# Attention's loads in another order: v one group of heads later, q and k one group sooner

## The chip, the cores and the metric

One core of a Trainium2 chip runs the whole program. The metric is the device time of one execution in microseconds; three runs of the kernel before are given below, and one more was taken by the hardware profiler.

## What is computed

The reference is an attention with sigmoid in place of softmax, followed by a maximum over three products and an output product:

```python
def _attn_ref(q, k, v):                      # 8 batches, 12 heads, 448 positions, 64 wide
    S = q.shape[2]
    scores = np.matmul(q, k.transpose(0, 1, 3, 2)) / np.sqrt(q.shape[-1]) - np.log(S)
    attn = 1.0 / (1.0 + np.exp(-scores))
    return np.matmul(attn, v)

def _moe_ref(x, w1, w2, w3, w_out):          # x: 3584 tokens of 768; weights 768 x 768
    h = np.maximum(np.maximum(x @ w1, x @ w2), x @ w3)
    return h @ w_out
```

## The kernel before, in words

The program has two stretches. The first, `attention` (lines 238 to 410), works through 24 groups of four heads: `fours` (line 335) lists 8 batches by 3 groups. A group has two pairs of heads; each pair has one tile qk of 128 partitions by 896 (two heads of 64 rows, q and k side by side), 448 KB. All four heads share one tile v of 448 KB. The second stretch (lines 416 to 555) does the four products in a Strassen-like scheme of seven block products, operands split in two float32r parts (`PRODUCTS`, `product`); its weights are decoded from 64-bit words, a part of them during attention.

Most instructions are pinned to program order (`pin`), so each engine's row is the order in which the code is written. One turn n of attention's loop (lines 365 to 408) puts these in the rows:

- SP (the load and store queue): `load(n + 1)`, that is the two qk tiles (line 270) and then v (line 275) of the next group; the raw weight words of a later decode, wraw (line 134); in half of the decodes a store of the decoded words, w_dram (line 173); from turn 9 on, for twelve turns, a block of attention's own output, xs (line 190); at the end the two stores of the finished group, x_dram (line 350).
- TensorE: `last_scores` of group n (line 313; positions 384 to 447 of all four heads, read from the unsplit qk tiles), the three score chunks of the first pair (line 301; two go to ps_s, the third to ps_av through `accumulator`), the three chunks of the second pair (all to ps_s), and then the weighing of group n - 1 with v: 24 matmuls of `weigh` (line 321) and 8 of `last_weigh` (line 330), all into ps_av.
- ScalarE: a sigmoid of each score chunk (line 280; the tile is named last for `last_scores`, else a), with the two steps of one weight decode (lines 144 and 145) between the first and the second pair.
- VectorE: up to two weight splits (lines 122 and 123), `qk_split` of the next group's first pair (hi, line 289, and lo, line 290), the decode's four steps (lines 146 to 155), `qk_split` of the next group's second pair, and the copies m of group n - 1 out of ps_av (line 349), which the stores of line 350 wait for.
- GpSimd: sums of weight blocks (line 110) and of x blocks (line 199).

Group 0 is different: its first pair isn't split, and its turn has two calls of `decode`, of which the first only issues the first two wraw loads.

Buffers decide when a load can go. There are four qk tiles (line 242), that is two groups, and two v tiles (line 244). There is one ps_av, so the third chunk of a group can't be written until the copies m of the group weighed before have read it, and the weighing can't begin until the third chunk's sigmoid has. There are three ps_s tiles, and two each of hi and lo, which the scores of a pair hold to their end. A load that has to wait for its buffer stands in SP's row, and what is behind it stands too. In `load(n + 1)` the qk tiles are those of group n - 1, which was last read at the beginning of turn n - 1; the v tile is that of group n - 1, which is weighed at the end of turn n.

Of the kernel before, what the change touches and what calls it, by code (L numbers as in the profile page):

```python
# [34 lines left out]
def attention_then_maxout(  # L35
# [84 lines left out]
    def w_split(q, name, r, copy):  # L120
        hi, lo = w_tiles(q, name)
        pin(copy(out=hi, in_=r[name]))
        pin(nc.vector.tensor_tensor(out=lo, in0=r[name], in1=hi.bitcast(F32), op=ALU.subtract))
# [59 lines left out]
    def x_block(r, src, p, row, th, k=None):  # L183

        name = f"b{row + 1}{th + 1}"
        if name not in r:
            r[name] = xs_tile(name)
        ks = slice(0, HALF) if k is None else slice(k, k + 1)
        t = (2 * p + th) * S
        pin(nc.sync.dma_start(out=r[name][:, ks], in_=src[row][:, ks, t : t + S]))  # L190

    def x_combine(r, names=TOKENS, ks=range(HALF)):

        for name in names:
            if name not in r:
                r[name] = r["b12"] if name == "t3" else xs_tile(name)
            in0, in1 = SUMS[name]
            for k in ks:
                pin(nc.gpsimd.tensor_tensor(  # L199
                    out=r[name][:, k], in0=r[in0][:, k], in1=r[in1][:, k], op=ALU.subtract  # L200
                ))
# [8 lines left out]
    def t_store(r, p, names=TOKENS):  # L210
        for name in names:
            k = TOKENS.index(name)
            pin(nc.sync.dma_start(out=t_dram[p][:, k], in_=r[name]))
# [13 lines left out]
    def x_hi(name, r):  # L227
        hi = xo_p[name not in FIRST].tile([P, HALF, S], F32R, name=f"xhi_{name}")
        lo = xo_p[name not in FIRST].tile([P, HALF, S], F32R, name=f"xlo_{name}")
        pin(nc.scalar.copy(out=hi, in_=r[name]))  # L230
        return name, r[name], hi, lo

    def x_lo(name, x, hi, lo):
        pin(nc.vector.tensor_tensor(out=lo, in0=x, in1=hi.bitcast(F32), op=ALU.subtract))  # L234
        x_ops[name] = hi, lo


    def attention(stack):
# [15 lines left out]
        def decode():  # L254
            done = next(background)
            if done:
                q, stage = done
                decoded.append(q)
                if decoded.count(q) == len(BLOCKS):
                    splits.extend((q, name, stage) for name, _, _ in PRODUCTS)  # L260
# [3 lines left out]
        def load_qk(b, k):  # L264
            t = qk_p.tile([P, 2 * S], F32, name="qk")
            if b == k == 0:
                pin(nc.scalar.dma_start(out=t[D:], in_=qk[b, k, D:]))
                pin(nc.sync.dma_start(out=t[:D], in_=qk[b, k, :D]))
            else:
                pin(nc.sync.dma_start(out=t, in_=qk[b, k]))  # L270
            return t

        def load_v(b, f):
            t = v_p.tile([P, 14, D], F32, name="v")
            pin(nc.sync.dma_start(out=t, in_=v[b, f]))
            return t

        def sigmoid(ps, **kw):
            a = a_p.tile([P, 2, S], F32, name="last" if kw else "a", **kw)
            pin(nc.scalar.activation(  # L280
                out=a, in_=ps[:, :, :S], func=AF.Sigmoid, bias=bias_s, scale=scale
            ))
            return a

        def qk_split(t):

            hi = hl_p.tile([P, 2 * S], F32R, name="hi")
            lo = hl_p.tile([P, 2 * S], F32R, name="lo")
            pin(nc.vector.tensor_copy(out=hi, in_=t))  # L289
            pin(nc.vector.tensor_tensor(out=lo, in0=t, in1=hi.bitcast(F32), op=ALU.subtract))  # L290
            return (hi, hi), (hi, lo), (lo, hi)

        def accumulator():
            return ps_av.tile([P, 2, 512], F32, name="ps_av")

        def scores(terms, c, ps=None):
            ps = ps_s.tile([P, 2, 512], F32, name="ps_s") if ps is None else ps
            for n, (kt, qt) in enumerate(terms):
                for e in range(2):
                    r = slice(e * D, (e + 1) * D)  # L300
                    pin(nc.tensor.matmul(
                        ps[:, e, :S], kt[r, S + c * P : S + (c + 1) * P], qt[r, :S],
                        start=n == 0, stop=n == len(terms) - 1,
                    ))
            return sigmoid(ps)

        def last_scores(ts):

            ps = ps_s.tile([P, 2, 512], F32, name="ps_s")
            for g, t in enumerate(ts):  # L310
                for e in range(2):
                    r = slice(e * D, (e + 1) * D)
                    pin(nc.tensor.matmul(
                        ps[g * D : (g + 1) * D, e, :S], t[r, S + C * P :], t[r, :S],
                        start=True, stop=True,
                    ))
            return sigmoid(ps, bufs=2)

        def weigh(ps, vt, g, c, a):
            for e in range(2):  # L320
                pin(nc.tensor.matmul(  # L321
                    ps[e * D : (e + 1) * D, g, :S], vt[:, (g * C + c) * 2 + e], a[:, e],
                    start=c == 0, stop=False,
                ))

        def last_weigh(ps, vt, a):
            for g in range(2):
                r = slice(g * D, (g + 1) * D)
                for e in range(2):
                    pin(nc.tensor.matmul(  # L330
                        ps[e * D : (e + 1) * D, g, :S], vt[r, 4 * C + e], a[r, e],
                        start=False, stop=True,
                    ))

        fours = [(b, f) for b in range(B) for f in range(NK // 2)]
        loads = {}

        def load(n):
            if n < len(fours):
                b, f = fours[n]  # L340
                ts = load_qk(b, 2 * f), load_qk(b, 2 * f + 1)
                loads[n] = ts, load_v(b, f)

        def finish(n, ps, pool=m_p, names=("m11", "m12")):
            b, f = fours[n]
            for g in range(2):
# [5 lines left out]
                ))  # L352

        load(0)

        warm = const.tile([P, 1], F32, name="warm")
        pin(nc.scalar.activation(out=warm, in_=bias_s, func=AF.Sigmoid))
# [3 lines left out]
            r = slice(e * D, (e + 1) * D)  # L361
            pin(nc.tensor.matmul(ps[:, e, :P], idle[r], idle[r], start=True, stop=True))
        before, xs = None, {}
        terms = [(loads[0][0][0],) * 2], None
        for n in range(len(fours) + 1):
            if n < len(fours):
                load(n + 1)
                ts, vt = loads.pop(n)
                if n:
                    last = last_scores(ts)  # L370
                    for _ in range(2):
                        if splits:
                            w_split(*splits.pop(0), nc.vector.tensor_copy)
                first = [scores(terms[0], c, accumulator() if c == C - 1 else None)
                         for c in range(C)]
                if n == 0:
                    terms = None, qk_split(ts[1])
                    last = last_scores(ts)
                ahead = loads[n + 1][0] if n + 1 < len(fours) else None
                after = [qk_split(ahead[0]) if ahead else None]  # L380
                decode()
                second = [scores(terms[1], c) for c in range(C)]
                after.append(qk_split(ahead[1]) if ahead else None)
                terms = after
                if n == 0:
                    decode()
            else:
                for name in FIRST:
                    x_lo(*x_hi(name, xs))

            part = n - 9
            if 0 <= part < 4 * HALF:
                k, block = divmod(part, 4)
                row, th = ((0, 1), (0, 0), (1, 1), (1, 0))[block]
                x_block(xs, x_dram, 0, row, th, k)
                x_combine(xs, ((), ("t1",), ("t2", "t3"), ())[block], (k,))
            if n == len(fours) - 1:
                t_store(xs, 0, TOKENS[:3])
            if before:
                pvt, chunks, rest = before  # L400
                ps = accumulator()
                for g in range(2):
                    for c in range(C):
                        weigh(ps, pvt, g, c, chunks[g][c])
                last_weigh(ps, pvt, rest)
                if n < len(fours):
                    finish(n - 1, ps)
            before = vt, (first, second), last
# [3 lines left out]
    with ExitStack() as stack:  # L412
        xs, finish = attention(stack)
# [183 lines left out]
```

## Time and profile before

| | |
|---|---|
| time, median of 3 runs | 935.5 us (933.01, 935.5, 942.13) |
| profiled execution | 941.3 us, its span (first to last instruction) 939.5 us |
| TensorE busy | 893.5 us of the span |
| VectorE, ScalarE, GpSimd busy | 621.5, 394.4, 181.7 us |
| mean granted TensorE clock | 0.98 |
| moved by DMA | 161.87 MB, mean 172 GB/s |

Busy time is a share over both stretches, which have different limits, so it says little by itself; the time of a stretch and what each engine waits for in it say more. Times in rows count from the span's start.

### The profile page before, as it was taken

The numbers are of one execution on the slowest core, as the hardware profiler recorded it, in microseconds if no ns is written. First come the engines' busy times: TensorE is split into PE (matmuls) and PEld (weight loads), VectorE is DVE, ScalarE is ACT, GpSimd is POOL, SyncE is SP. The second block draws the span as 40 slices with busy tenths as digits, with TensorE's granted clock in tenths as the row PEclk, the third lists the DMA queues.
The fourth block names the chain that finished last, engine by engine and source line by source line (L and its number), as shares of the span: only waits on it lengthen the run. The fifth ranks groups of instructions, "written<-read, shape, count | busy, mean of one in ns | idle before, by whom it ended". The sixth has DMA issues, their size and how long they took to land. (4 is left out here: it accounts for less than half of the span.)

```text
span 939.5 us, 12879 instructions
## 1 busy us (share of the span) xinstructions
PE 893.5 (95%) x4866; PEld 715.9 (76%) x4866; DVE 621.5 (66%) x875; ACT 394.4 (42%) x499; POOL 181.7 (19%) x148
## 2 busy tenths in 40 slices
PE   8888888889988999999999999999999999999998
PEld 4553444444544599999999999999999998989997
DVE  5465555555466656757968688878786877756352
ACT  6555655556554522404324234224351443514220
POOL 0100012010110163280110001020001072841500
PEclk9989999999999999999999999999999999999999
DMA  5564546665565466361383663255727324451522
GB/s 190 190 200 149 199 165 210 226 196 183 173 208 164 164 247 229 127 235 62 102 310 119 236 235 139 93 174 217 271 89 290 116 84 139 150 206 69 177 79 78
DMA packets 74350, 161.87 MB, mean 172 GB/s; under 512 B 6960, under 2 KB 53808, under 8 KB 74288
## 3 DMA queue, kind: packets, MB, share of 16 engines
q1 hardware_dynamic: 74208, 160.82, 48.9%
q8 instruction: 38, 0.62, 0.3%
q10 hardware_dynamic: 80, 0.23, 0.1%
q14 instruction: 24, 0.20, 0.1%
HBM read 109.90 MB, written 51.12 MB: 171 GB/s over the span
## 5 line engine op out<-in xcount | busy, mean ns | idle before, releaser
L427 PE MATMUL ps_y<-xhi_t,wlo_s 128*128 128x448 f32 x432 | 158.1, 366 | 1.3 <-ACT xhi_b L230 1.3
L427 PE MATMUL ps_y<-xhi_t,whi_s 128*128 128x448 f32 x432 | 158.0, 366 | 0.0
L427 PE MATMUL ps_y<-xlo_t,whi_s 128*128 128x448 f32 x432 | 158.0, 366 | 0.0
L280 ACT ACTIVATE a<-ps_s,bias_s 128x896 f32<-128x896 f32 x120 | 112.8, 1003 | 27.6 <-PE ps_av L321 22.6
L321 PE MATMUL ps_av<-a,v 128*64 128x448 f32 x576 | 115.4, 550 | 1.4 <-issue 1.3
L427 PE MATMUL ps_y<-xhi_b,wlo_a 128*128 128x448 f32 x288 | 105.4, 366 | 0.0
L427 PE MATMUL ps_y<-xlo_b,whi_a 128*128 128x448 f32 x288 | 105.3, 366 | 0.0
L427 PE MATMUL ps_y<-xhi_b,whi_a 128*128 128x448 f32 x288 | 105.3, 366 | 0.0
L289 DVE CAST hi<-qk 128x896 fp32r<-128x896 f32 x47 | 29.3, 623 | 114.9 <-DMA qk<-qk 97.8
L110 POOL TENSOR_TENSOR ws_s<-ws_a,ws_a 128x384 f32<-128x384 f32 x12 | 14.3, 1190 | 434.3 <-DMA ws_a<-w_dram 230.7
L522 ACT COPY p<-ps_y 128x448 f32<-128x448 f32 x48 | 25.5, 532 | 163.9 <-PE ps_y L427 163.9
L321 PEld LDWEIGHTS ps_av<-a,v 128*64 128x64 f32 x576 | 40.1, 139 | 67.2 <-issue 62.7
L427 PEld LDWEIGHTS ps_y<-xhi_t,wlo_s 128*128 128x128 f32 x432 | 81.1, 188 | 8.3 <-ACT xhi_b L230 1.6
L427 PEld LDWEIGHTS ps_y<-xlo_t,whi_s 128*128 128x128 f32 x432 | 81.1, 188 | 6.7
L427 PEld LDWEIGHTS ps_y<-xhi_t,whi_s 128*128 128x128 f32 x432 | 81.1, 188 | 6.7
L496 DVE TENSOR_TENSOR m<-ps_y,u 128x448 f32<-128x448 f32 x72 | 44.7, 621 | 59.6 <-PE ps_y L427 58.4
L199 POOL TENSOR_TENSOR xs_t<-xs_b,xs_t 128x448 f32<-128x448 f32 x48 | 62.5, 1327 | 54.9 <-DVE wb L154 43.0
L525 DVE TENSOR_TENSOR u<-ps_y,p 128x448 f32<-128x448 f32 x48 | 29.9, 623 | 57.8 <-PE ps_y L427 56.7
L234 DVE TENSOR_TENSOR xlo_t<-xs_t,xhi_t 128x1344 fp32r<-128x1344 f32 x42 | 67.9, 1617 | 0.0
L234 DVE TENSOR_TENSOR xlo_b<-xs_b,xhi_b 128x1344 fp32r<-128x1344 f32 x42 | 66.6, 1587 | 0.0
L494 ACT COPY m<-ps_y 128x448 f32<-128x448 f32 x24 | 12.8, 534 | 127.5 <-PE ps_y L427 123.9
L230 ACT CAST xhi_t<-xs_t 128x1344 fp32r<-128x1344 f32 x42 | 55.5, 1321 | 16.0 <-PE ps_y L427 9.7
(78 smaller groups left out, 1725.5 us busy)
## 6 DMA issues: line engine op xcount, KB each, us to landing
qk<-qk SPq DMA_DIRECT2D x47, 448.0 KB, 5.3
xs_b<-x_dram SPq DMA_DIRECT2D x30, 672.0 KB, 6.9
wraw<-w SPq DMA_DIRECT2D x36, 384.0 KB, 4.5
xs_t<-t_dram SPq DMA_DIRECT2D x18, 672.0 KB, 7.9
v<-v SPq DMA_DIRECT2D x24, 448.0 KB, 3.4
h_dram<-m SPq DMA_DIRECT2D x48, 224.0 KB, 1.9
xs_b<-h_dram SPq DMA_DIRECT2D x16, 672.0 KB, 6.1
outT<-m SPq DMA_DIRECT2D x48, 224.0 KB, 1.9
```

Source lines behind the costliest of these rows:

```text
L110: pin(nc.gpsimd.tensor_tensor(out=r[name], in0=r[in0], in1=r[in1], op=op))
L199: pin(nc.gpsimd.tensor_tensor(out=r[name][:, k], in0=r[in0][:, k], in1=r[in1][:, k], op=ALU.subtract))
L230: pin(nc.scalar.copy(out=hi, in_=r[name]))
L234: pin(nc.vector.tensor_tensor(out=lo, in0=x, in1=hi.bitcast(F32), op=ALU.subtract))
L280: pin(nc.scalar.activation(out=a, in_=ps[:, :, :S], func=AF.Sigmoid, bias=bias_s, scale=scale))
L289: pin(nc.vector.tensor_copy(out=hi, in_=t))
L321: pin(nc.tensor.matmul(ps[e * D : (e + 1) * D, g, :S], vt[:, (g * C + c) * 2 + e], a[:, e], start=c == 0, stop=False,))
L427: pin(nc.tensor.matmul(ps[:, :S], wt[:, k * P : (k + 1) * P], xt[:, k], start=first and n == 0, stop=n == len(terms) - 1, skip_group_check ...
L494: pin(nc.scalar.copy(out=m[name], in_=y))
L496: pin(nc.vector.tensor_tensor(out=m[name], in0=y, in1=add, op=ALU.add))
L522: pin(nc.scalar.copy(out=p1, in_=ps[0][:, :S]))
L525: pin(nc.vector.tensor_tensor(out=u2, in0=ps[1][:, :S], in1=p1, op=ALU.add))
```

## The change

The group's qk tiles are loaded two groups ahead instead of one, and v not ahead but in the turn of its own group. In turn n the two qk loads of group n + 2 come after `last_scores(ts)` of group n in the code, which is the last reader of the buffers that they take; v of group n follows, into the buffer that the weighing at the end of turn n - 1 has left. At the start the qk tiles of groups 0 and 1 are loaded without v; in turn 0 v comes first, and then the qk tiles of group 2.

```diff
         def load(n):
             if n < len(fours):
                 b, f = fours[n]
-                ts = load_qk(b, 2 * f), load_qk(b, 2 * f + 1)
-                loads[n] = ts, load_v(b, f)
+                loads[n] = load_qk(b, 2 * f), load_qk(b, 2 * f + 1)
...
         load(0)
+        load(1)
...
-        terms = [(loads[0][0][0],) * 2], None
+        terms = [(loads[0][0],) * 2], None
         for n in range(len(fours) + 1):
             if n < len(fours):
-                load(n + 1)
-                ts, vt = loads.pop(n)
+                ts = loads.pop(n)
                 if n:
                     last = last_scores(ts)
+                    load(n + 2)
+                    vt = load_v(*fours[n])
...
                 if n == 0:
                     terms = None, qk_split(ts[1])
                     last = last_scores(ts)
-                ahead = loads[n + 1][0] if n + 1 < len(fours) else None
+                    vt = load_v(*fours[n])
+                    load(n + 2)
+                ahead = loads.get(n + 1)
```

The rows of TensorE, VectorE, ScalarE and GpSimd stay as they are; SP's row alone is in another order. The names are tiles with a running number, which differs between the two programs; x_dram0 and x_dram1 are the two halves of attention's output.

At the program's start SP's row changes so (- before, + now):

```order
 L268 DMA qk_120<-qk 64x896
 L270 DMA qk_123<-qk 128x896
-L275 DMA v_125<-v 128x896
-L270 DMA qk_142<-qk 128x896
-L270 DMA qk_144<-qk 128x896
-L275 DMA v_146<-v 128x896
-L134 DMA wraw_178<-w123 128x384
+L270 DMA qk_125<-qk 128x896
+L270 DMA qk_127<-qk 128x896
+L275 DMA v_170<-v 128x896
+L270 DMA qk_172<-qk 128x896
+L270 DMA qk_174<-qk 128x896
```

v of group 0 has moved behind the qk tiles of group 1, v of group 1 has left this place, and the qk tiles of group 2 (qk_172 and qk_174) now stand in front of the first two wraw loads.

In the middle of attention, SP's row of turn 9 and the beginning of turn 10 before, with the counters that each waits for in brackets (PE is TensorE's, DVE VectorE's, Activation ScalarE's, DMAHW that of an earlier transfer):

```order
L270 DMA qk_1132<-qk 128x896 [waits DMAHW5_49]
L270 DMA qk_1134<-qk 128x896 [waits DMAHW6_49]
L275 DMA v_1136<-v 128x896 [waits DMAHW7_49,PE_49]
L134 DMA wraw_1176<-w123 128x384 [waits DMAHW0_49,Activation_49]
L190 DMA xs_b12_1219<-x_dram0_64 128x448 [waits DMAHW1_49]
L350 DMA x_dram1_65<-m11_1238 128x448 [waits DMAHW2_49,DVE_49]
L350 DMA x_dram1_65<-m12_1241 128x448 [waits DMAHW3_49,DVE_49]
```

And the same turn now:

```order
L270 DMA qk_1141<-qk 128x896 [waits DMAHW6_49,PE_49]
L270 DMA qk_1143<-qk 128x896 [waits DMAHW7_49,PE_49]
L275 DMA v_1145<-v 128x896 [waits DMAHW0_49]
L134 DMA wraw_1178<-w123 128x384 [waits DMAHW1_49,Activation_49]
L190 DMA xs_b12_1221<-x_dram0_64 128x448 [waits DMAHW2_49]
L349 DMA x_dram1_65<-m11_1240 128x448 [waits DMAHW3_49,DVE_49]
L349 DMA x_dram1_65<-m12_1243 128x448 [waits DMAHW4_49,DVE_49]
```

The order of kinds is the same; what moved is the group that a load belongs to, and with it the wait: v waited for TensorE (the weighing at the end of this turn) and now doesn't, the qk tiles now do (`last_scores` at its beginning).

## Rows read from the trace of the kernel before

**Rows 1.** Busy time of the engines in three stretches of the span (the start, attention from the first group's last_weigh to the 23rd's, the products): stretch, its length, then for each engine busy us and instructions, the mean granted clock as a share of full speed, the DMA engines' busy share, GB/s.

```profile
0.00:24.32 24.32, 21.40 (x131) 11.17 (x131) 13.16 (x20) 16.42 (x20) 1.52 (x5) 1.00 0.54 184
24.32:308.96 284.64, 248.66 (x1674) 135.16 (x1672) 162.15 (x258) 164.26 (x199) 28.11 (x22) 0.93 0.56 187
316.84:939.50 622.66, 616.87 (x3028) 567.24 (x3024) 439.41 (x592) 208.87 (x277) 149.86 (x120) 1.00 0.46 163
```

The engines' columns are PE (TensorE's matmuls), PEld (its weight loads), DVE (VectorE), ACT (ScalarE), POOL (GpSimd).

**Rows 2.** What TensorE's matmuls waited for between 24.3 and 309 us: us in total, times, longest.

```profile
PE ps_av L301 <- DVE m L349: 35.6, 14, 4.0
```

**Rows 3.** Instructions in order of time, from the end of one group's weighing to the third score chunk two groups on: start in us, busy us, engine, line, operation, output and inputs, count; in brackets the idle time before it and what ended it.

```profile
113.71 0.33 SPq L275 DMA_DIRECT2D v<-v  x1
115.91 1.15 DVE L349 COPY m<-ps_av 128x448 f32<-128x448 f32 x2
116.55 0.86 SPq L350 DMA_DIRECT2D x_dram<-m  x2
117.20 0.47 PE L301 MATMUL ps_av<-hi 64*128 64x448 f32 x2 [1.37 <-DVE m L349]
117.46 0.92 SPq L270 DMA_DIRECT2D qk<-qk  x2
...
122.55 0.63 DVE L289 CAST hi<-qk 128x896 fp32r<-128x896 f32 x1 [5.50 <-DMA qk<-qk]
123.22 1.09 DVE L290 TENSOR_TENSOR lo<-qk,hi 128x896 fp32r<-128x896 f32 x1
...
124.49 0.98 PE L330 MATMUL ps_av<-last,v 64*64 64x448 f32 x8
126.54 1.32 POOL L110 TENSOR_TENSOR ws_s<-ws_a,ws_a 128x384 f32<-128x384 f32 x1 [75.81 <-DVE ws_a L155]
127.03 1.78 DVE L290 TENSOR_TENSOR lo<-qk,hi 128x896 fp32r<-128x896 f32 x1
128.73 1.14 DVE L349 COPY m<-ps_av 128x448 f32<-128x448 f32 x2
130.02 0.74 PE L301 MATMUL ps_av<-hi 64*128 64x448 f32 x2 [2.38 <-DVE m L349]
```

**Rows 4.** The same view as rows 2 for VectorE, between 24.3 and 309 us.

```profile
DVE hi L289 <- DMA qk<-qk: 91.2, 19, 8.6
```

**Rows 5.** The view of rows 1 for single groups, each from the start of its last_weigh to that of the next group's (columns as in rows 1).

```profile
24.32:34.55 10.23, 10.23 (x78) 5.44 (x76) 2.85 (x5) 7.40 (x9) 0.00 (x0) 1.00 0.64 218
...
124.49:138.83 14.34, 11.96 (x78) 6.97 (x76) 9.74 (x16) 7.50 (x9) 2.15 (x2) 0.88 0.50 171
...
166.13:176.34 10.21, 10.21 (x78) 5.42 (x76) 3.62 (x7) 6.97 (x9) 0.00 (x0) 1.00 0.77 256
...
244.82:255.43 10.61, 10.45 (x78) 5.56 (x76) 3.13 (x4) 7.40 (x9) 4.12 (x3) 1.00 0.68 232
255.43:271.82 16.39, 12.40 (x79) 7.29 (x77) 14.53 (x22) 7.50 (x9) 3.58 (x3) 0.90 0.45 151
...
298.75:308.96 10.21, 10.21 (x78) 5.42 (x76) 4.86 (x9) 7.46 (x10) 1.52 (x2) 1.00 0.49 153
```

**Rows 6.** The last of these groups in order of time (columns as in rows 3).

```profile
298.75 0.98 PE L330 MATMUL ps_av<-last,v 64*64 64x448 f32 x8
...
299.80 1.16 DVE L349 COPY m<-ps_av 128x448 f32<-128x448 f32 x2 [0.21 <-PE ps_av L330]
...
303.23 1.02 ACT L280 ACTIVATE a<-ps_av,bias_s 128x896 f32<-128x896 f32 x1
...
304.30 4.73 PE L321 MATMUL ps_av<-a,v 128*64 128x448 f32 x24
305.20 0.56 ACT L144 ACTIVATE c<-wraw 128x384 f32<-128x384 f32 x1 [0.95 <-DMA wraw<-w]
305.67 0.55 ACT L145 ACTIVATE wraw<-wraw 128x384 uint32<-128x384 uint32 x1
...
306.12 2.79 ACT L280 ACTIVATE a<-ps_s,bias_s 128x896 f32<-128x896 f32 x3
...
307.39 0.56 DVE L155 SCALAR_TENSOR_TENSOR wb<-c,wb 128x384 f32<-128x384 f32 x1
...
308.96 0.98 PE L330 MATMUL ps_av<-last,v 64*64 64x448 f32 x8
```

**Rows 7.** What SP's queue itself waited for between 24.3 and 309 us (us in total, times, longest).

```profile
SPq L275 <- PE ps_av L330: 167.8, 22, 13.2
```

**Rows 8.** The start in order of time (columns as in rows 3).

```profile
4.64 0.91 SPq L134 DMA_DIRECT2D wraw<-w  x2
...
11.32 0.80 SPq L270 DMA_DIRECT2D qk<-qk  x2
...
14.97 0.57 ACT L144 ACTIVATE c<-wraw 128x384 f32<-128x384 f32 x1
...
15.87 1.04 ACT L280 ACTIVATE last<-ps_s,bias_s 128x896 f32<-128x896 f32 x1
...
16.96 0.47 PE L301 MATMUL ps_s<-hi 64*128 64x448 f32 x2 [0.32 <-ACT last L280]
...
24.32 0.98 PE L330 MATMUL ps_av<-last,v 64*64 64x448 f32 x8
```

**Rows 9.** The view of the tile wraw, up to 320 us: time from a load's issue to its landing.

```profile
DMA to landing us min/median/max: 3.2/4.4/8.4
```

## Prediction

> **What bounds the kernel now.** I read by stretches first. Attention's steady part, from the first group's last weighing to the 23rd's, lasts 284.64 us; TensorE is busy 248.66 us of it at a mean granted clock of 0.93. The products after it (316.84 us to the end) have it busy 616.87 of 622.66 us at 1.00 [rows 1]. So something is lost in attention and next to nothing behind it; what attention gives back moves the end by as much, as long as the products need nothing that comes at a fixed time. They don't: their operands come from VectorE, ScalarE and loads that are issued in attention's own order.
>
> Second, who is waited for: in this stretch TensorE waits 35.6 us in 14 places, all of them the third score chunk of a group, which is written to ps_av, and all for VectorE's copy m out of ps_av [rows 2]. Third, why the copy is late, in time order. The weighing of a group ends just before 113.7 us; v's load is issued at that moment, since its buffer was held until then, but the copy starts at 115.91, behind VectorE's split. Its two stores go out at 116.55 and only then, at 117.46, the next q and k, which land for the split at 122.55, after 5.50 us of an idle VectorE. One group on, the weighing ends at 125.47 (124.49 + 0.98), VectorE is still splitting, the copy starts at 128.73, and TensorE, idle for 2.38 us, goes on at 130.02 [rows 3]. It is a ring: late copy, late store, late load, late split, late copy. In all, VectorE waits 91.2 us for q and k [rows 4].
>
> **What the ring costs.** Of the 22 groups in the stretch, eight have no wait of TensorE for the copy; they take 10.21 to 10.23 us each (first and last shown), 81.74 us together. The 14 others take 284.64 - 81.74 = 202.90 us, against 14 x 10.22 = 143.08: 59.8 us too much. Only 35.6 us of that is the wait itself; the other 24.2 us is slower running after it. The group from 124.49 shows it: 14.34 us with 11.96 us of busy PE where an unhindered group has 10.21, at a granted clock of 0.88 [rows 5]. After that stop the engine runs for a while on its lower level, 1.2 of 2.4 GHz: one matmul row lasts 0.74 us where the same row had 0.47 before [rows 3]. So a stall of 2.38 us costs 4.1.
>
> **The change part by part.** No engine but SP gets another order; no instruction is added or taken away, the bytes are the same. Five things to work out.
>
> (1) q and k one group sooner. They are still issued behind the stores of the copy, at the same place of the ring, but they are the pair for the group after next. The pair that the split wants was issued a whole group (10.2 us) before; at the landing of 5.1 us (117.46 to 122.55 [rows 3]) it lies ready some 5 us ahead. VectorE's wait of 91.2 us falls to about 0. The new wait is that a buffer is free only when last_scores has read it; that is the first thing TensorE does in a group, and SP stands behind the copy's stores at that time anyway. Cost: 0 in steady state, covered by these stores.
>
> (2) What is late next? VectorE's row in a group ends with the second split, in front of the copy. In the unhindered group from 298.75 (weighing ends at 299.73) the third sigmoid ends at 304.25, ScalarE could do the two decode steps at once (1.02 us: 305.20 to 306.22), until 305.27; VectorE's last decode step ended 1.73 us after ScalarE's (307.95 against 306.22), so 307.0; the split, whose buffer the second half's scores have left by 304.30, takes 1.76 us (0.63 + 1.09 and gaps, as at 122.55 in [rows 3]), so 308.8. The weighing ends at 309.94: 1.2 us to spare [rows 6]. VectorE's total load fits as well: the two heaviest neighbouring groups hold 3.13 + 14.53 = 17.66 us of it, 8.8 a group [rows 5]. TensorE then sets the pace: 22 x 10.22 = 224.8 us. Gain 59.8 us; bounds 35.6 (only the waits go, the clock stays as poor) and 59.8 (nothing in the rows allows a group under 10.21). I take 59.8, since all eight groups without a wait ran at 10.21 to 10.23 and a clock of 1.00.
>
> (3) v one group later. Its buffer is free at once, so SP no longer stands at it: 167.8 us of waiting go [rows 7], and the decode's raw words behind it are asked for earlier. v is wanted a group and a half after its issue. Gain on the path: none beyond (1).
>
> (4) The start pays. In front of the first two wraw loads (issued at 4.64) there are now the q and k of the third group, which wait for the first last_scores; before, they were issued at 11.32. So wraw goes out at about 12.2 instead and lands 4.4 us later (median; 3.2 to 8.4) [rows 8, 9], at 16.6. ScalarE stands at this decode from 14.97 on; behind it in order is the sigmoid of last, for whose buffer TensorE already waits 0.32 us at 16.96 [rows 8]. Shift: 16.6 - 14.97 = 1.6 us; bounds 0.4 (landing 3.2) and 5.6 (8.4). TensorE then stands idle for some 2 us, about the 2.38 after which the clock fell: half of that group's extra 1.75 us, 0.9.
>
> (5) VectorE beside GpSimd. Where GpSimd began a sum 0.49 us ahead of a split's subtraction (126.54 and 127.03), that lasted 1.78 us instead of 1.09 [rows 3]: 0.7 us lost. Shorter groups make such meetings no rarer. I cost them at 0, since one of them fits in the 1.2 us to spare; three in one group, as the groups from 244.82 and 255.43 hold [rows 5], would lose 2.1 and put the copy 0.9 us late: that is rival A. The Trainium skill ("SBUF — State Buffer", Who interferes with whom) has a harder rule: a VectorE instruction with two SBUF inputs is blocked for the whole of a GpSimd instruction that reads SBUF. By it a sum of 1.32 us [rows 3] could cost all of its 1.32, three of them 4.0 us, and the copy of such a group would be 2.8 us late instead of 0.9.
>
> **Sum.** 941.3 us (the profiled execution: span 939.5 and 1.8 around it) - 59.8 + 1.6 + 0.9 = 884.0 us. The median of the runs, 935.5, is 5.8 us lower than the profiled execution; I read that as a matter of how many groups stalled, and since the sum is built from groups without stalls I don't scale it.
>
> **Rivals.**
> A. VectorE becomes late by its own work: decode, weight splits and GpSimd's sums meet in some groups, and the copy is late again. For: only 1.2 us to spare, worked out and not seen. Against: 8.8 us of work in the heaviest pair. Price: 22 GpSimd instructions in the stretch [rows 1], at two or three in a group some 9 groups; each 0.9 us late, and half of them with the clock's 1.75: 9 x 0.9 + 4.5 x 1.75 = 16, so 900. By the Trainium skill's rule under (5) the first term would be 9 x 2.8 = 25 and the time 917.
> B. The transfers don't keep the pace. Attention moves 187 GB/s x 284.64 / 22 = 2.42 MB a group; in 10.22 us that is 237 GB/s and a DMA share of 0.56 x 284.64 / 224.8 = 0.71. Against: one 10.21 us group moved 256 GB/s at 0.77. For: others moved 218 at 0.64. If 218 were the limit a group would take 11.1 us: 22 x 0.9 = 20 more, 904.
> C. Slower: wraw late in every group. SP now has q and k (waiting for TensorE) and v ahead of it in one rush, and ScalarE's decode stands in order before the second half's sigmoids. Issued at copy start (299.80) + 0.64 + 0.86 + 0.92 + 0.33 + gaps, about 303.0, it is wanted at the next group's 304.25 + 10.22, 11.5 us later; ScalarE can be 2.0 us late before it holds anything up (the group's last sigmoid ended at 308.91 with the decode 0.95 late, 1.03 before the weighing's end [rows 6]). So it decides from a landing of 13.5 us on, and from 16.2 (59.8 / 22 = 2.7 more) the kernel is slower than before; at 17 us it is 884 + 22 x 3.5 = 961. Against: the longest landing of wraw in attention is 8.4 us [rows 9].
> D. It doesn't do what it says: q and k stay late, since their issue stays where it is in SP's order. Then 941. Against: a group's lead can't vanish unless landing takes over 10 us.
>
> **How the numbers follow.** Forecast 884: 0.75; A 0.12; B 0.06; C 0.04; D 0.03. The forecast's own range is 878 to 890 (start cost 0.4 to 5.6, and a median some us below a profiled run). The range reaches to A and B, 877 to 905. A change of about 1% is what a measurement of this kernel can tell from none. Faster by more: forecast, A and B, 0.93; within: D, 0.03; slower: C, 0.04.
>
> **What would show it.** Right: TensorE's wait for m gone or under 4 us; granted clock near 1.00 up to 310 us, but for a dip near 18 us; last_weigh every 10.2 us; hi no longer waits for DMA; ScalarE waits about 1.6 us for wraw near 15 us; products' stretch unchanged at about 622.7 us. Wrong: m still waited for while VectorE is busy (A), hi or the decode waiting for DMA in each group (B, C), or a product stretch that grew by what attention lost.

## The result, and the profile after

| | before | after |
|---|---|---|
| median of six runs | 941.7 us (933.01 to 945.94) | 891.92 us (884.0 to 893.17) |
| profiled execution, its span | 941.3, 939.5 us | 893.17, 891.4 us |

The ratio is 0.946, 95% interval 0.9398 to 0.9522. The forecast was 884.0, its own range 878 to 890, the range with its rivals 877 to 905.

The three stretches of [rows 1], cut at the same events in the changed kernel (first last_weigh, 23rd last_weigh, first product):

```profile
0.00:27.09 27.09, 21.40 (x131) 12.30 (x131) 13.17 (x20) 16.25 (x20) 1.53 (x5) 0.94 0.62 214
27.09:252.45 225.36, 225.24 (x1675) 118.57 (x1673) 162.63 (x258) 164.02 (x199) 28.98 (x23) 1.00 0.69 234
260.33:891.40 631.07, 625.77 (x3028) 567.11 (x3024) 437.34 (x592) 209.29 (x277) 148.96 (x120) 1.00 0.45 161
```

The 22 groups now take 225.36 us, 10.24 each, with TensorE busy throughout at a granted clock of 1.00. The other two stretches became longer: the start by 2.8 us, the products by 8.4.

TensorE waits for nothing between 27.1 and 252.4 us. What VectorE waited for there (us in total, times, longest), beside [rows 4]:

```profile
DVE m L348 <- PE ps_av L330: 35.3, 22, 2.1
DVE hi L289 <- PE ps_av L301: 16.8, 12, 1.6
DVE wb L154 <- ACT wraw L145: 2.5, 1, 2.5
```

The direction has turned round: the copy m waits for the weighing, in all 22 groups, where the third score chunk's ps_av waited for the copy. Rows picked from one group in order of time, beside [rows 3], and the copy that was nearest to late:

```profile
109.06 0.98 PE L330 MATMUL ps_av<-last,v 64*64 64x448 f32 x8
110.11 1.16 DVE L348 COPY m<-ps_av 128x448 f32<-128x448 f32 x2 [1.26 <-PE ps_av L330]
110.76 0.85 SPq L349 DMA_DIRECT2D x_dram<-m  x2
111.70 0.91 SPq L270 DMA_DIRECT2D qk<-qk  x2
112.03 0.37 PE L301 MATMUL ps_av<-hi 64*128 64x448 f32 x2
112.85 0.63 DVE L289 CAST hi<-qk 128x896 fp32r<-128x896 f32 x1 [1.58 <-PE ps_av L301]
116.68 0.62 DVE L289 CAST hi<-qk 128x896 fp32r<-128x896 f32 x1
119.30 0.98 PE L330 MATMUL ps_av<-last,v 64*64 64x448 f32 x8
...
222.82 1.16 DVE L348 COPY m<-ps_av 128x448 f32<-128x448 f32 x2 [0.89 <-PE ps_av L330]
```

The q and k issued at 111.70 are not those that the split at 112.85 reads; that split now waits only until the first pair's scores have left its buffer. VectorE is ready 1.26 us before the copy can start, at the least 0.89.

### The profile page after: what moved, and what is told of

It is laid out like the page before. It is cut to its first block, busy times and chain, and to the rows that moved or that the text cites. A ratio compares the mean times of both kernels' runs of the same rounds, so it can differ in the third digit from the quotient of the medians.

```text
span 891.4 us, 12898 instructions
## 1 busy us (share of the span) xinstructions
PE 879.0 (99%) x4866; PEld 700.3 (79%) x4866; DVE 620.0 (70%) x875; ACT 393.6 (44%) x499; POOL 180.0 (20%) x148
## 5 line engine op out<-in xcount | busy, mean ns | idle before, releaser
L321 PE MATMUL ps_av<-a,v 128*64 128x448 f32 x576 | 113.5, 543 | 1.4 <-issue 1.3
L230 ACT CAST xhi_t<-xs_t 128x1344 fp32r<-128x1344 f32 x42 | 55.6, 1323 | 16.1 <-PE ps_y L430 12.5
L144 ACT ACTIVATE c<-wraw 128x384 f32<-128x384 f32 x48 | 27.0, 562 | 77.9 <-DVE m L505 47.5
```

Source lines behind the costliest of these rows:

```text
L144: pin(nc.scalar.activation(out=square, in_=high.bitcast(F32), func=AF.Square))
L321: pin(nc.tensor.matmul(ps[e * D : (e + 1) * D, g, :S], vt[:, (g * C + c) * 2 + e], a[:, e], start=c == 0, stop=False,))
```

## Experiments

Each is the changed or the former kernel with one edit. "Lead" is the time from a load's issue to the instruction that wants it.

**q and k sooner alone.** v is loaded one group ahead as before, so SP's queue stands for it again.

```diff
                     last = last_scores(ts)
                     load(n + 2)
-                    vt = load_v(*fours[n])
+                    vt = vs.pop(n)
+                    next_v(n + 1)            # vs[n + 1] = load_v(*fours[n + 1])
```

> q and k two groups ahead as in the changed kernel, v as in the kernel before (one group ahead, its load standing in SP's row until the weighing at the end of the turn). Theory (the ring copy - store - q and k load - split is broken by q's and k's lead alone): groups of 10.2 to 10.3 us, TensorE's wait for m under 4 us, 885 to 898 us; the raw weight words come up to 1 us late on ScalarE without effect. Rival (the release of SP's queue from v's wait is what pays): TensorE waits for m as before, 925 to 942 us.

885.77 us (883.35 to 892.75), ratio to the kernel before 0.9408 (0.9346 to 0.947). What SP's queue and TensorE waited for between 27.3 and 253 us:

```profile
SPq L275 <- PE ps_av L330: 144.2, 22, 13.3
```

```profile
PE ps_av L301 <- DVE m L348: 0.6, 1, 0.6
```

SP stands for v for 144.2 us, as it did for 167.8 before [rows 7]. The 22 groups take 226.14 us all the same, 0.8 more than in the changed kernel, and one copy is late, by 0.6 us. The lead of q and k alone gives the whole gain in time; the rival falls. What SP's standing costs here is room:

```profile
DVE m L348 <- PE ps_av L330: 10.4, 12, 2.4
```

VectorE is ahead of the weighing in 12 groups and by 10.4 us in all, where it was in 22 and by 35.3 in the changed kernel.

**v later alone.** v comes in its own group's turn, q and k one group ahead.

```diff
-                load(n + 1)                  # q, k and v of the next group
+                load(n + 1)                  # q and k only
                 ...
                     last = last_scores(ts)
+                    vt = load_v(*fours[n])
```

> v in the turn of its own group as in the changed kernel, q and k one group ahead as before, still behind the stores of the copy. Theory (ring through q and k): VectorE still waits some 80 to 90 us for q and k, TensorE some 30 us for m, 925 to 945 us. Rival (v's wait in SP's queue is what made the loads late): 885 to 898 us.

910.83 us (907.1 to 917.51), ratio 0.967 (0.9604 to 0.9735): neither. What TensorE and VectorE waited for between 24.1 and 279 us:

```profile
PE ps_av L301 <- DVE m L348: 22.9, 18, 3.1
```

```profile
DVE hi L289 <- DMA qk<-qk: 71.5, 19, 6.3
```

The 22 groups (columns as in [rows 1]):

```profile
24.01:279.16 255.15, 232.28 (x1675) 123.93 (x1673) 161.66 (x258) 165.22 (x199) 31.31 (x23) 0.99 0.62 211
```

The ring is still there, in 18 groups instead of 14, but its stops are shorter: 255.15 us for the 22 groups against 284.64. Of the 29.5 us between them 12.7 are TensorE's wait for m (35.6 to 22.9); most of the rest is the clock, which is granted at 0.99 here and at 0.93 before. So my theory of the ring lacked a part. The kernel before has it, in the group from 138.83:

```profile
138.83 0.98 PE L330 MATMUL ps_av<-last,v 64*64 64x448 f32 x8
139.88 0.33 SPq L275 DMA_DIRECT2D v<-v  x1
140.30 0.38 SPq L134 DMA_DIRECT2D wraw<-w  x1
141.25 0.86 SPq L350 DMA_DIRECT2D x_dram<-m  x2
142.15 1.61 SPq L270 DMA_DIRECT2D qk<-qk  x2
149.87 0.63 DVE L289 CAST hi<-qk 128x896 fp32r<-128x896 f32 x1 [8.60 <-DMA qk<-qk]
...
157.57 0.94 SPq L270 DMA_DIRECT2D qk<-qk  x2
161.37 0.63 DVE L289 CAST hi<-qk 128x896 fp32r<-128x896 f32 x1 [1.51 <-DMA qk<-qk]
```

When the copy was in time, v and wraw (832 KB), released at the weighing's end, and a block xs went out just before q and k, and these were 7.7 us under way (142.15 to 149.87); a group later the copy was late, v and wraw were through by then, and it took 3.8 us. I read this as the reason why short and long groups mostly alternated before: a group in time prepared the next one's delay. With v behind q and k 15 of the 22 groups take 10.75 to 12.2 us, four 10.2 to 10.3 and three 13.6 to 14.5.

**v in front of q and k.** To separate transfer order from SP's standing, v of v_later's order was put in front of q and k; SP waits for it no more than 0.4 us in all.

```diff
+                vt = load_v(*fours[n])
                 load(n + 1)
                 ...
                     last = last_scores(ts)
-                    vt = load_v(*fours[n])
```

> As v_later (v in the turn of its own group, q and k one group ahead behind the stores), but v's load in front of q's and k's instead of behind. SP's queue stands nowhere for v. Theory (in the kernel before, v and wraw, released at the weighing's end, travel in front of q and k, whose landing takes up to 8 us; v_later won its 33 us by letting q and k travel first): q and k land some 1.3 us later than in v_later (448 KB more in front), groups of about 12.5 us, 925 to 945 us. Rival (v_later won by SP's queue no longer standing, that is by earlier wraw): 905 to 918 us as v_later.

946.62 us (937.49 to 949.9), ratio 1.0074 (1.0029 to 1.0119). TensorE's and VectorE's waits between 24 and 308 us:

```profile
PE ps_av L301 <- DVE m L348: 39.6, 20, 4.0
```

```profile
DVE hi L289 <- DMA qk<-qk: 100.4, 19, 7.2
```

```profile
23.59:308.04 284.45, 244.86 (x1675) 135.11 (x1673) 161.53 (x258) 165.56 (x199) 31.33 (x23) 0.93 0.56 189
```

VectorE's wait grew by 28.9 us, 1.3 us a group, and the 22 groups took 284.45 us, 1.3 a group more than with v behind; in that the lower clock (0.93 against 0.99) is included. The rival falls; the time lies 1.6 us above the range that was expected, with groups of 12.9 us where 12.5 were. One load of 448 KB in front of q and k costs a group 1.3 us. The loads are as late here as before although SP doesn't stand for v, so its standing is not needed for the ring.

**q and k ahead of the stores.** The lead made shorter than a group, with nothing else between copy and load.

```diff
                     last = last_scores(ts)
-                    load(n + 2)
                     vt = load_v(*fours[n])
                 ...
+            load(n + 2)                      # for every n; turn 0's own load(n + 2) goes too
             if n == len(fours) - 1:          # the weighing and its copy and stores follow
```

> The changed kernel with the q and k loads of group n + 2 at the end of turn n, ahead of the copy's stores and not behind the last_scores of the turn; so they are issued some us before the copy and lead by less than a group, and the first wraw loads stand in front of them. Theory (what counts is that the q and k that a split wants don't hang on the copy before it; any lead over their landing will do): groups of 10.2 to 10.3 us, TensorE waits under 4 us for m, 878 to 893 us, the start as fast as with the wraw loads first. Rival (a whole group of lead is needed): VectorE waits for q and k in each group, TensorE for m, 900 us or more.

879.58 us (879.05 to 886.51), ratio 0.9392 (0.9327 to 0.9458). In turns with a store of decoded weights SP reaches the load late, as here:

```profile
50.72 0.88 SPq L270 DMA_DIRECT2D qk<-qk  x2
...
56.62 0.62 DVE L289 CAST hi<-qk 128x896 fp32r<-128x896 f32 x1
```

```profile
22.03:247.44 225.41, 225.33 (x1674) 118.65 (x1672) 161.38 (x258) 164.06 (x199) 29.84 (x23) 1.00 0.71 234
```

A lead of 5.9 us is enough: no wait for DMA at 56.62, 225.41 us for the 22 groups, TensorE waits for nothing in them. Not a whole group of lead is needed but one over the landing.

**The first wraw loads first.** The start's cost undone.

```diff
                     vt = load_v(*fours[n])   # n == 0
-                    load(n + 2)
                 ...
                 decode()                     # its first call issues two wraw loads
+                if n == 0:
+                    load(n + 2)
```

> The changed kernel with the first two raw weight loads in front of the third group's q and k, as before. Theory (those loads, held by the wait for the first last_scores, cost the start 2.8 us): the first last_weigh starts at 24.3 us instead of 27.1, ScalarE doesn't wait for wraw in the first 20 us, groups still 10.2 us, the end of attention's weighing 2.8 us earlier; the time 2 to 3 us under the changed kernel's at the same pace of the products. Rival (the start was lost to q's and k's other order in the transfers): first last_weigh near 27 us again.

880.55 us (879.8 to 883.6), ratio 0.9351 (0.9292 to 0.9411). First the start of the changed kernel in order of time, beside [rows 8], with the clock of 19 to 21 us (0.50), then that of this version:

```profile
9.34 0.98 PE L313 MATMUL ps_s<-qk 64*64 64x448 f32 x8
10.35 0.80 SPq L270 DMA_DIRECT2D qk<-qk  x2
11.20 0.90 SPq L134 DMA_DIRECT2D wraw<-w  x2
...
17.03 0.56 ACT L144 ACTIVATE c<-wraw 128x384 f32<-128x384 f32 x1 [2.83 <-DMA wraw<-w]
17.93 1.00 ACT L280 ACTIVATE last<-ps_s,bias_s 128x896 f32<-128x896 f32 x1
18.98 0.74 PE L301 MATMUL ps_s<-hi 64*128 64x448 f32 x2 [3.23 <-ACT last L280]
...
27.09 0.98 PE L330 MATMUL ps_av<-last,v 64*64 64x448 f32 x8
```

```profile
19.00:21.00 2.00, 2.00 (x10) 1.81 (x12) 1.97 (x4) 2.00 (x3) 0.00 (x0) 0.50 0.98 340
```

```profile
4.00 0.91 SPq L134 DMA_DIRECT2D wraw<-w  x2
7.92 0.98 PE L313 MATMUL ps_s<-qk 64*64 64x448 f32 x8
12.80 0.59 ACT L144 ACTIVATE c<-wraw 128x384 f32<-128x384 f32 x1
22.14 0.98 PE L330 MATMUL ps_av<-last,v 64*64 64x448 f32 x8
```

The first last_scores itself starts anywhere from 7.55 to 10.2 us in the traces, so the cost is read from there to the first last_weigh: 14.12 us before (10.20 to 24.32), 17.75 in the changed kernel (17.28 and 18.66 in the two further traces of it, below), 14.22 with wraw first (14.15 when run again). The start costs the change 3.6 us, 3.2 and 4.5 by the further traces, and this edit gives it back; the rival, q's and k's order in the transfers, falls.

**The same two again.** The changed kernel was run twice more and this version once more.

> The changed kernel again, for the spread of its runs (884 to 893 us in six) and the pace of the products' matmuls, which in its trace was 206.7 ns for most of the stretch, in the trace of before 202.7 ns for most. Theory (the pace of a long row of matmuls takes one of two values by chance of the execution, not by the change): runs on both sides, near 884 and near 892, and a trace whose share of the slow pace agrees with its time by 4 ns a matmul. Rival (the change itself makes the products slower, by later or colliding loads): the slow pace in the same stretches again, all runs near 892.

> The changed kernel a third time, beside start_wraw_2. Theory (two paces by execution): 883 to 893 us; the first weighing starts about 17.8 us after the first last_scores; attention's 22 groups in 225.4 us; the products' stretch of the trace is 622 us plus 4 ns for each matmul at the slow pace over those of the trace of before. Rival (the product stretch depends on the change): a product stretch that doesn't follow from the pace.

> The version with the first wraw loads in front of the third group's q and k again, beside the changed kernel on one chip. Theory (the start costs the change about 3.6 us, clock included): 878 to 888 us, by the products' pace, and 2 to 5 us under the changed kernel at the same pace; the first weighing starts about 14.2 us after the first last_scores, as in the kernel before. Rival (its lower times were a fast pace by chance): the same median as the changed kernel within 2 us.

The changed kernel gave 886.93 us (883.48 to 891.39) and 888.66 (882.89 to 892.95), ratios 0.9411 (0.9354 to 0.9468) and 0.9487 (0.9406 to 0.9569); wraw first gave 888.36 (887.1 to 888.55), ratio 0.9466 (0.9409 to 0.9523). By medians, then, the second comparison of the two shows no difference: as the rival has it. The traces say why. Busy time in 40 us of the products: the changed kernel's first trace, its second, the second of wraw first, and the kernel before (columns as in [rows 1]; the count behind PE's time is what to look at):

```profile
340.33:380.33 40.00, 40.00 (x195) 36.34 (x194) 26.91 (x33) 11.69 (x12) 19.50 (x16) 1.00 0.51 183
```

```profile
340.33:380.33 40.00, 40.00 (x199) 37.08 (x199) 27.54 (x32) 11.28 (x11) 20.33 (x16) 1.00 0.52 186
```

```profile
340.33:380.33 40.00, 40.00 (x195) 36.34 (x194) 29.18 (x31) 11.27 (x11) 19.83 (x16) 1.00 0.50 179
```

```profile
396.84:436.84 40.00, 40.00 (x199) 37.07 (x198) 28.36 (x32) 11.42 (x12) 20.27 (x16) 1.00 0.53 188
```

One and the same program does 195 matmuls in 40 us in one execution and 199 in another, with no wait and a clock of 1.00 in both. Averaged over 10 us without a stop or a change of pace, the matmuls' starts are 206.7 or 202.7 ns apart; the single distances are 206 and 207 ns at the slower pace, and at the faster go round between 199 and 207. The changed kernel's traces at 202.7 ns through most of the products had 883.48 and 882.89 us, the one at 206.7 ns 893.17; wraw first had 879.8 at 202.7 and 888.55 at 206.7. At equal pace wraw first is thus 3.1 to 4.6 us faster; the medians show it in the first series (880.55 against 886.93) and not in the second, where all four runs of wraw first took 887 to 889 us. The expectation of runs near 884 and near 892 holds only in part: two of the four runs of the second series of the changed kernel lie between, at 886.61 and 887.24.

## Why the prediction was right, and where it was not

| term, from profiled execution to profiled execution | predicted | measured |
|---|---|---|
| 22 groups of attention | -59.8 | -59.3 (284.64 to 225.36) |
| start | +2.5 | +2.8 (24.32 to 27.09) |
| products | 0 | +8.4 |
| sum, from 941.3 | 884.0 | 893.2 |

**(1) and what the ring costs.** Held: the wait of 91.2 us for q and k is gone, TensorE's 35.6 us too, and the other 24.2 us with them. That the full 59.8 and not only the waits' 35.6 would come was the choice that mattered. Groups take 10.24 instead of 10.22 us. But the 24.2 us were not all slower running: the mean clock of 0.93 over 284.64 us [rows 1] takes about 20 us, and the clock record of the trace, which stands at 0.50 for 37.5 us, 35.5 of them with TensorE busy, some 18. A stop without a fall of the clock also costs 0.2 us beyond the wait (the group from 244.82 in [rows 5] has 10.61 - 10.22 - 0.16), some 3 us over 14 stops; and in a few groups `last_scores` itself was late, since its weight loads waited for q and k (the kernel before, 24.3 to 309 us):

```profile
PEld ps_s L313 <- DMA qk<-qk: 2.6, 4, 0.8
```

The total was right because it was taken from groups that ran without all of these.

**(2) What is late next.** Nothing. 1.2 us to spare were worked out; the copies had 0.89 to 2.1. Rival A did not come: the split's subtraction was slowed to about 1.78 us in nine places, as before, one in a group and not two or three, and each fitted in. The blocking that the prediction weighed (the Trainium skill, "SBUF — State Buffer", section "Who interferes with whom") cost no group anything either. All nine meetings look like this one:

```profile
116.90 1.26 POOL L110 TENSOR_TENSOR ws_s<-ws_s,ws_a 128x384 f32<-128x384 f32 x1 [9.00 <-DVE ws_a L155]
117.33 1.78 DVE L290 TENSOR_TENSOR lo<-qk,hi 128x896 fp32r<-128x896 f32 x1
```

The sum has 0.82 to 0.83 us to go when the subtraction begins, and the subtraction loses 0.68 to 0.69. That is most of what was left of the sum; a loss of all of its 1.32 us, which the prediction priced, would need the two to begin together, and none of the nine did. So the runs decide between rule and row only that far.

**(3) v.** Right for the change as a whole: with q and k sooner, v's place is worth no time that the runs show, only room for VectorE. Wrong as a picture of the ring: the landing of q and k was taken as one number, 5.1 us, and it is made by what travels in front of it. By itself v's place is worth 33 us by the medians (910.83 against 943.7), and the two parts' gains don't add: 58 for q and k, 33 for v, 57 for both.

**(4) The start.** The mechanism held, the size was small: wraw landed 5.8 us after its issue (11.20 to 17.03), not 4.4, with 896 KB of q and k in front of it; TensorE stood 3.23 us, not 2, and the clock did fall (0.50), where half was put down for it. The cost is 3.6 us from the first last_scores on (3.2 and 4.5 in the other traces), against 2.5.

**B, C and D.** The stretch moved 234 GB/s (237 worked out) at a share of 0.69 without a wait for a transfer in steady state; ScalarE waited for wraw once, at the start. q and k were late nowhere in it.

**The step that failed** is "products' stretch unchanged at about 622.7 us". The slow pace held from 271 to 738 and from 782 to 883 us in the profiled execution, 568 us or some 2,750 matmuls at 4.0 ns: 11.0 us. In the trace of before it held from 830 to 931 us: 2.0. That makes 9.0 of the 8.4 us measured; the rest, below zero, lies mostly in shorter stops between stages (TensorE idle for 5.3 us of the stretch, 5.8 before). All ten traces fit: from the first start of a product's matmul to the last, less 4 ns for each matmul at the slower pace, they have 615.5 to 617.5 us. Since the same program runs either way, the change is not needed for the slower pace, and the version with v in front of q and k, these one group ahead as before, has it from 326 to 797 us; whether the change makes it more frequent isn't shown, for the kernel before was traced only once. The forecast's 884 is the time at the faster pace: the two traces of the changed kernel at that pace had 883.48 and 882.89 us. In part that is luck, since the one trace that the sum began from ran at the faster pace for most of its products. The median, 891.92, lies outside the forecast's own 878 to 890; it lies inside the wider range only because that reaches to A and B, which did not come. What sets the pace stays open. It changes at short stops of TensorE in most places (near 270 and 782 us), but also without one (738 us here, 350 us in the trace of q and k sooner alone), and no run here was made to force it.

The fastest version is the one with q and k ahead of the stores, 879.58 us beside 888.66 for the changed kernel in the same series; by traces at one pace (879.05 against 882.89) 3.8 us of that come with its start, which has wraw first as well, and the rest agrees with the pace.

## What to carry to other kernels

A wait shown for a transfer may be a ring: the load hangs on a store that hangs on the work that the load makes late. Look at what a late load's issue stands behind, and break the ring by a lead over the landing time; here more lead than that gave nothing. Compute the gain from the iterations that already run without the stall, since they leave out all that the stall takes with it, the clock above all. What is issued just in front of a load is part of its landing time, so put what is wanted last, last, at the start above all.

## What the runs showed of the hardware that was not expected

A long row of 128x448 matmuls, each with its own weights, has two paces here, 202.7 and 206.7 ns on average from start to start, at the same granted clock of 1.00, by execution and by stretch of one execution: 9 to 10 us of this kernel (893.17 against 883.48, 888.55 against 879.8). A load of 448 KB in front of q and k on the same queue delayed them by 1.3 us a group. And a stop of TensorE for 2.4 to 4 us came with its lower clock, 0.50, in nine of ten groups of the kernel before, but not in all: after 3.33 us at 94.01 the matmuls ran at once at 1.00.
